# Early picks in one stretch, a plain first slot, K of the third pair over two queues, and one late unit's values in a score buffer

## Chip, cores and metric

The kernel runs on one core of one Trainium2 chip. The metric is the time of one execution on the device in microseconds (us), the median of several runs. Five engines work side by side, each with its own instruction order, and wait for each other through semaphores: PE (TensorE: matmuls into the PSUM accumulators), DVE (VectorE), ACT (ScalarE), POOL (GpSimd) and SP (SyncE, which here only starts transfers). A transfer can be started from the queue of SP, ACT or POOL, and stands there in the same order as that engine's other instructions.

## What is computed

Attention with queries pooled in pairs, and behind it a top-1 mixture of experts. q, k and v are 8 x 8 x 1152 x 64 in float32; there are 8 experts with an inner width of 1024.

```python
q_pool = q.reshape(B, H, S // 2, 2, D).mean(axis=3)          # 576 queries
scores = np.matmul(q_pool, k.transpose(0, 1, 3, 2)) / np.sqrt(D)
attn = np.exp(scores - np.max(scores, axis=-1, keepdims=True))
attn = attn / (np.sum(attn, axis=-1, keepdims=True) + 1e-09)
x = heads_joined(np.matmul(attn, v))                         # 4608 tokens x 512
expert_idx, gate_w = top1(softmax(x @ w_gate))
for e in range(8):
    out[expert_idx == e] = gate_w * (np.maximum(x @ w1[e], 0.0) @ w2[e])
```

## The kernel before

**Attention.** The work is 8 batches x 4 pairs of heads x 2 halves of the queries: 64 units, eight in each batch. For a pair, `load_pair` (L476) loads K (`kp`, four transfers of 144 KB), Q (`qn`) and V (`vn`). Two neighbouring queries are added (`qp`, on POOL at L527 for all pairs but the first), and DVE transposes K and Q in blocks (`kT` L537, `qT` L541). A unit's scores are nine chunks: PE writes one into a score buffer (`st`, L573; there are three such buffers in PSUM), and DVE takes it out with its maximum (L577, a "take"). Behind the ninth chunk come `top` (L598), a small spread on PE (L595) and the `bias` (L601); then ACT makes the exponentials (L605) in five pieces. POOL folds the exponentials for the row sums (L665), PE adds up what is left (L648, L655), and PE multiplies the exponentials by V (`values`, L709) into the one value buffer `pa`. ACT and DVE bring `pa` into `xT` (L715, L717).

**Start.** For the first two pairs (`start`), half of the K and Q transfers go over the queue of ACT (`side`, L488) and half over SP; for all others all go over SP (L487). Every such transfer start waits for one of eight semaphores, which SP and ACT use in turn: a start waits until the transfer that had its semaphore last has landed.

**Routing and slots.** When a batch is done, `routing` (L757) turns its row sums (L725, L732), makes the logits (L787), brings them over on ACT (L808, `sm`), turns them back (L794), weighs them (`lw`, L800) and finds each token's expert. The tokens then go through 16 slots, each for one expert: three early slots, six wide and seven static ones. Behind the next-to-last batch `first_slots` (L911) chooses the three early slots' experts: three picks of twelve small DVE instructions each (L931 to L942). Each pick has a score buffer of its own for its scratch row (`pe`), and in the plan the picks stand some time apart (`K_NEXT * i`).

**A slot.** `turn_tokens` (L1176) weighs gathered tokens (`xt`, L1196), crosses them on PE into `px` (L1204), and splits them into a rounded part `xh` (ACT, L1211) and a rest `xl` (DVE, L1152). `split_weights` (L1230) does so with the weights (`w1h`, `w1l`, `w2h`, `w2l`; casts on ACT at L1243, rests on DVE at L1152). `first_products` (L1261) makes eight blocks of twelve matmuls (L1305) in two buffers `ph`, each emptied into `hh` (ACT, L1313) and `hl` (DVE, L1315), and `second_products` (L1321) multiplies these by `w2` into `py` (L1335).

The first slot is special. The first of its eight blocks is made in three parts (`by_part`, L1291): four matmuls that need only `xh` and `w1h`, four that need also `xl`, and four that need `w1l`. A filler (L1281) keeps PE busy ahead of them. The third cross goes into `py`, so that it doesn't wait for a `px`. Casts of the weights behind the first wait for the `xh`, rests for the `xl`; the logits of the last batch wait for the parts.

**Order.** All of this is laid out by a planner (`Flow`, L95) ahead of time: steps have a key, an estimated duration, steps that must come before them and buffers that they hold, and the planner writes out one fixed order for each engine. A change of a key or a buffer thus changes the order of other work too.

Of the kernel before, what the change touches and what calls it, by code (L numbers as in the profile page):

```python
# [9 lines left out]
F32 = mybir.dt.float32  # L10
# [60 lines left out]
FILLERS = 1  # L71
# [198 lines left out]
def kernel(  # L270
# [151 lines left out]
    def open_attention(exact, base, pairs, units):  # L422
# [10 lines left out]
        o.turned, o.asked, o.gate, o.ended = [], None, None, []  # L433
# [42 lines left out]
    def load_pair(o, f, key, b, hp):  # L476
# [13 lines left out]
        start = not o.exact and b == 0 and hp < 2  # L490

        def quarters(t, src, n0=0, n1=rows, load=load):

            for h in range(2):
                for i in range(D // BL):
                    g = (h * D // BL + i) * BL
                    (side if start and h else load)(t[g:g + BL, n0:n1], src[h][:, i * BL:(i + 1) * BL].rearrange("(p n) d -> p n d", p=BL)[:, n0:n1])

        def k_part(n0, n1, ns, move, after=()):
            return f.carry("SP", ns, lambda: quarters(kp.t, heads(k, b, hp), n0, n1), key + K_LOAD, after, [kp], move)  # L500

        def q_part(n0, n1, ns, move):
            return f.carry("SP", ns, lambda: quarters(
                qn.t.rearrange("p j b t d -> p (j b t) d"), heads(q, b, hp), n0, n1),
# [191 lines left out]
    def values(o, f, key, x, s, ready, hp, half, xT):  # L696
        pa = value_banks(o)
# [18 lines left out]
        o.ended += done(a)  # L716
# [27 lines left out]
    def attend(o, f, key, b, hp, xT, sm, summed):  # L744
# [3 lines left out]
        for half in range(2):  # L748
# [3 lines left out]
            outs.append(values(o, f, at + 10 - (40 if end and half else 0), x, s, r, hp, half, xT))  # L752
# [4 lines left out]
    def routing(o, f, key, b, xT, rec, ready, hold=()):  # L757
# [49 lines left out]
        o.logits = p = f.add("PE", 1050, logits, at, done(o.gate, *ready), [pl, xT], COLS)  # L807
        p = f.add("ACT", act(HQ) - 44, lambda: nc.scalar.copy(lg.t, pl.t[:, 0, :HQ]), at, done(p), [pl, lg])  # L808
# [58 lines left out]
        def put(g):  # L867
# [18 lines left out]
            p = [f.add("ACT", 115, lambda d=d: spread(d), at + K_SPREAD, ready, [rec, row]) for d in range(NQD)]  # L886
            p += [f.add("DVE", dve(NR * P), lambda j=j: turn(j), at + K_PUT * j / NJ / NB, ready, [row, xT]) for j in range(0, NJ, NR)]
# [23 lines left out]
    def first_slots(o, m, f, key, ready):  # L911
# [7 lines left out]
        n, pl8 = small("fn"), small("fpl8")  # L919
        p = f.add("PE", 60, lambda: nc.tensor.matmul(pc.t[0:1, 0, :NE], ones_bf[:, 0:1], cnt, start=True, stop=True),  # L920
# [5 lines left out]
        def pick(i, p):  # L926

            pe = score_banks(o)
            eq = lambda: pe.t[0:1, 1, :NE]
# [577 lines left out]
```

## Time and profile before

| | |
|---|---|
| median of 3 runs | 1147.12 us (1146.98 to 1150.65) |
| the profiled execution | 1160.67 us, of which the span is 1159.0 us |
| PE busy | 1121.1 us, 97% of the span |
| DVE, POOL, ACT busy | 882.6, 846.7 and 619.8 us |
| attention of the 64 units | from the start to about 683 us |
| slots | from about 684 us to the end |

The profiled execution is 13.55 us longer than the median. Times in it are read from its own start; sums of them are set against its own time.

### The profile page before, as it was taken

How to read it: one execution, taken by the hardware profiler on the slowest of the kernel's cores; microseconds unless marked ns; L12 is line 12 of the kernel's file. 1: busy time of each engine (PE TensorE's matmuls, PEld its weight loads, DVE VectorE, ACT ScalarE, POOL GpSimd, SP SyncE). 2: the span in 40 equal slices, each digit the busy share in tenths (PEclk: the TensorE clock that was granted, in tenths of full speed). 3: DMA queues.
4: the chain of work that ended last, by engine and by line, in shares of the span. 5: the costliest groups of instructions: out<-in, count | busy, mean ns of one | idle time of the engine just before them, and what ended most of it. 6: DMA issues, size and time to landing. Idle time of an engine off the chain costs nothing.

```text
span 1159.0 us, 32925 instructions
## 1 busy us (share of the span) xinstructions
PE 1121.1 (97%) x13237; PEld 797.0 (69%) x13237; DVE 882.6 (76%) x2245; ACT 619.8 (53%) x831; POOL 846.7 (73%) x484
## 2 busy tenths in 40 slices
PE   7999999999999999999999989999999999999994
PEld 3555555555555655555555568899999999899894
DVE  7988988989989889898889849755665556677760
ACT  2755656556557456555555555444444444555550
POOL 2999999999999999999999832766655654455510
PEclk9999999999999999999999999999999999999998
DMA  9876757566566566558453347856555555677630
GB/s 139 144 145 122 128 79 129 86 103 115 85 105 122 72 109 126 88 84 139 77 94 82 93 116 183 246 156 196 179 175 157 170 172 184 202 253 240 220 124 14
DMA packets 397977, 158.07 MB, mean 136 GB/s; under 512 B 314310, under 2 KB 368482, under 8 KB 397816
## 3 DMA queue, kind: packets, MB, share of 16 engines
q1 hardware_dynamic: 376696, 133.63, 52.9%
q0 software_dynamic: 10464, 20.78, 5.8%
q10 hardware_dynamic: 10656, 1.48, 1.1%
q8 instruction: 106, 1.74, 0.7%
q14 instruction: 55, 0.45, 0.1%
HBM read 135.02 MB, written 22.07 MB: 136 GB/s over the span
## 4 chain that ended last, share of the span: by engine, by line
PE 69%; DVE 16%; issue 6%; DMA 4%; POOL 2%; ACT 1%; SPq 1%; another core or an unknown queue 0%; POOLq 0%; DVEq 0%; ACTq 0%
PE st L573 18%; PE pa L709 17%; PE ph L1305 15%; PE py L1335 15%; DVE s L577 8%; PE st L655 2%; DMA vn<-in_v_dram 2%; DVE kT L537 2%; PE st L648 1%; DVE row L877 1%; POOL fold L665 1%; DMA qn<-in_q_dram 1%; PE st L595 1%; SPq L487 1%; POOL out_dram L1344 1%
## 5 line engine op out<-in xcount | busy, mean ns | idle before, releaser
L605 ACT ACTIVATE s<-s,bias 128x1152 f32<-128x1152 f32 (+1 forms) x320 | 352.0, 1152 | 242.2 <-DVE bias L601 218.3
L577 DVE TENSOR_SCALAR_CACHE_REDUCE s<-st 128x576 f32<-128x576 f32 x576 | 417.2, 748 | 48.4 <-PE st L573 33.1
L573 PE MATMUL st<-qT,kT 64*64 64x288 f32 x4608 | 366.3, 409 | 12.4 <-DVE s L577 7.8
L709 PE MATMUL pa<-s,vn 64*64 64x288 f32 x4608 | 350.1, 404 | 1.6 <-DVE xT L717 1.1
L573 PEld LDWEIGHTS st<-qT,kT 64*64 64x64 f32 x4608 | 165.1, 133 | 138.0 <-DVE s L577 57.0
L709 PEld LDWEIGHTS pa<-s,vn 64*64 64x64 f32 x4608 | 175.5, 133 | 105.9 <-issue 8.7
L665 POOL TENSOR_TENSOR fold<-s 128x1728 f32<-128x1728 f32 x55 | 213.0, 3874 | 17.4 <-ACT s L605 15.5
L665 POOL TENSOR_TENSOR fold<-fold,s 128x1728 f32<-128x1728 f32 x55 | 213.1, 3876 | 1.5
L1305 PE MATMUL ph<-xh,w1h 128*128 128x372 f32 (+1 forms) x508 | 155.7, 306 | 0.5 <-DVE hl L1315 0.5
L1305 PE MATMUL ph<-xl,w1h 128*128 128x372 f32 (+1 forms) x508 | 155.4, 306 | 0.0
L1305 PE MATMUL ph<-xh,w1l 128*128 128x372 f32 (+1 forms) x508 | 154.6, 304 | 0.0
L1152 DVE TENSOR_TENSOR w2l<-raw,w2h 128x1024 fp32r<-128x1024 f32 x64 | 78.1, 1224 | 84.9 <-ACT w2h L1243 76.1
L1021 POOL DMA_INDIRECT xr<-x_runs,ix x76 | 89.4, 1177 | 54.4 <-issue 24.8
L1335 PE MATMUL py<-w2h,hh 128*128 128x512 f32 x328 | 128.1, 391 | 0.0
L1335 PE MATMUL py<-w2h,hl 128*128 128x512 f32 x328 | 127.8, 390 | 0.0
L1335 PE MATMUL py<-w2l,hh 128*128 128x512 f32 x328 | 127.8, 390 | 0.0
L1313 ACT ACTIVATE hh<-ph 128x372 fp32r<-128x372 f32 (+1 forms) x100 | 51.1, 511 | 107.3 <-PE ph L1305 94.3
L1344 POOL DMA_INDIRECT out_dram<-y,rec x41 | 43.4, 1058 | 84.8 <-ACT y L1352 64.4
L1021 POOL DMA_INDIRECT xq<-x_runs,ix x52 | 63.4, 1219 | 49.0 <-PE py L1335 26.5
L1305 PEld LDWEIGHTS ph<-xh,w1h 128*128 128x128 f32 x508 | 95.4, 188 | 2.0 <-DVE hl L1315 0.8
L1305 PEld LDWEIGHTS ph<-xl,w1h 128*128 128x128 f32 x508 | 95.4, 188 | 0.6
L1305 PEld LDWEIGHTS ph<-xh,w1l 128*128 128x128 f32 x508 | 95.2, 187 | 0.0
(225 smaller groups left out, 1331.8 us busy)
## 6 DMA issues: line engine op xcount, KB each, us to landing
raw<-in_moe_w_dram SPq DMA_DIRECT2D x128, 512.0 KB
vn<-in_v_dram SPq DMA_DIRECT2D x124, 144.0 KB
kp<-in_k_dram SPq DMA_DIRECT2D x122, 144.0 KB
qn<-in_q_dram SPq DMA_DIRECT2D x120, 144.0 KB
x_runs<-row SPq DMA_DIRECT2D x96, 99.0 KB
xr<-x_runs,ix POOLq DMA_INDIRECT x76
x_runs<-empty SPq DMA_DIRECT2D x4, 297.0 KB
xq<-x_runs,ix POOLq DMA_INDIRECT x52
```

What stands on the lines that cost most here:

```text
L537: nc.vector.transpose(view(kT.t.rearrange(f"p (c b i) -> p {order} i", b=NQD, i=BL)), view(kp.t.rearrange(f"p ({order}) d -> p {order} d", ...
L573: nc.tensor.matmul(pt.t[to, h, :HQ], x.kT.t[up, c * P + i * D:c * P + (i + 1) * D], x.qT.t[up, cols], start=True, stop=True, tile_position ...
L577: nc.vector.tensor_scalar(s.t[:, c], pt.t[:, :, :HQ], -SCALE, None, op0=ALU.mult, op1=ALU.min, accum_out=mx.t[:, c:c + 1],)
L605: nc.scalar.activation(s.t[:, c0:c0 + n], s.t[:, c0:c0 + n], AF.Exp, bias=bias.t, scale=-1.0)
L665: add = lambda to, a, b: nc.gpsimd.tensor_tensor(to, a, b, ALU.add)
L709: mark.made = nc.tensor.matmul(pa.t[cs, i, :HQ], x.vn.t[up, h, c, :], s.t[up, c, h], start=c == 0, stop=c == NC - 1, tile_position=(up.sta ...
L1021: ins = nc.gpsimd.indirect_dma_start(out=x.xr[i // NQD].t[:, i % NQD, :], out_offset=None, in_=xg, in_offset=bass.IndirectOffsetOnAxis(ap= ...
L1152: (nc.gpsimd if eng == "POOL" else nc.vector).tensor_tensor(lo, raw, hi.bitcast(F32), ALU.subtract)
L1305: mark.made = nc.tensor.matmul(view()[:, i, :], a[:, c, fp], b[:, c, :n], start=c == 0 and k == 0, stop=c == NDC - 1 and k == 2)
L1313: a = f.add("ACT", act(nb * n) - 44, lambda home=home, apart=apart: nc.scalar.activation(home(0), apart(), AF.Relu), at - 20, done(p), [ph ...
L1335: mark.made = nc.tensor.matmul(py.t, blocks(a)[:, c * x.nr + r], b[:, c % 2, :], start=c == 0 and k == 0, stop=c == NFC - 1 and k == 2)
L1344: ins = nc.gpsimd.indirect_dma_start(out=out, out_offset=bass.IndirectOffsetOnAxis(ap=x.re.t.bitcast(I32)[:, r, 0:1], axis=0), in_=y.t, in ...
```

## The change

- **Picks.** The three picks write their scratch row into the buffer `pc` that holds the count they start from, and have one key.
- **First slot.** The parts, the filler, the third cross in `py` and the special waits are gone; all eight blocks are ordinary ones.
- **Third pair.** The transfers of K for the third pair (`third`: batch 0, pair 2) go half over ACT, half over SP. Its Q stays on SP.
- **Late values.** The values of the last unit go into a score buffer instead of `pa`.
- **Small things.** Two copies that pad `hh` and `hl` go from DVE to POOL, and the copies of the last batch's `rec` (L872) stand behind the copy of its logits (`copied`).

```diff
@@ load_pair
         start = not o.exact and b == 0 and hp < 2
+        third = not o.exact and b == 0 and hp == 2
...
-                    (side if start and h else load)(t[g:g + BL, n0:n1], src[h][:, i * BL:(i + 1) * BL].rearrange("(p n) d -> p n d", p=BL)[:, n0:n1])
+                    (side if both and h else load)(t[g:g + BL, n0:n1], src[h][:, i * BL:(i + 1) * BL].rearrange("(p n) d -> p n d", p=BL)[:, n0:n1])
 
         def k_part(n0, n1, ns, move, after=()):
-            return f.carry("SP", ns, lambda: quarters(kp.t, heads(k, b, hp), n0, n1), key + K_LOAD, after, [kp], move)
+            return f.carry("SP", ns, lambda: quarters(kp.t, heads(k, b, hp), n0, n1, start or third), key + K_LOAD, after, [kp], move)
...
-            move = 3800 if start else 4600 if not o.exact and b == 0 and hp == 2 else 2600
-            k0 = [k_part(0, rows, 620 if start else 1900, move, done(o.asked))] * 2
+            move = 3800 if start else 4600 if third else 2600
+            k0 = [k_part(0, rows, 620 if start else 950 if third else 1900, 3800 if third else move, done(o.asked))] * 2
@@ values, attend
-    def values(o, f, key, x, s, ready, hp, half, xT):
-        pa = value_banks(o)
+    def values(o, f, key, x, s, ready, hp, half, xT, banks):
+        pa = banks(o)
...
-            outs.append(values(o, f, at + 10 - (40 if end and half else 0), x, s, r, hp, half, xT))
+            outs.append(values(o, f, at + 10 - (40 if end and half else 0), x, s, r, hp, half, xT,
+                               score_banks if end and half else value_banks))
@@ routing
+            if b == B - 1:
+                f.order([copied], p)
@@ first_slots
+        eq = lambda: pc.t[0:1, 1, :NE]
...
-            pe = score_banks(o)
-            eq = lambda: pe.t[0:1, 1, :NE]
...
-            return f.add("DVE", 2300, lambda: [fn() for fn in fns], key + K_NEXT * i, done(p), [pe])
+            return f.add("DVE", 2300, lambda: [fn() for fn in fns], key, done(p), [pc])
@@ turn_tokens, split_weights, hidden
-                bank = "py" if x.begins and r == 2 else "px"
-                px = hold_of(bank, lambda h, bank=bank: m.ps.tile([P, DM], F32, **h.own(bank)))
+                px = hold_of("px", lambda h: m.ps.tile([P, DM], F32, **h.own("px")))
...
-            rows = x.casts if x.begins and (j or not one) else ()
-            lows = x.lows[:None if j or not one else 2] if x.begins else ()
...
-                nc.vector.tensor_copy(blocks(t)[:, :, RT:], ones4[:, 0, 0, 4:4 + P - RT].unsqueeze(1)
+                nc.gpsimd.tensor_copy(blocks(t)[:, :, RT:], ones4[:, 0, 0, 4:4 + P - RT].unsqueeze(1)
@@ first_products
-            if x.begins and f0 == 0:
...
-                p = f.add("PE", 430 * FILLERS, fill, at - 45, x.crossed, [filled])
...
-                    needs = ((*x.w1_ready[0][:1], *x.casts), x.lows, x.w1_ready[0])[k]
...
-            for i in range(0 if x.begins and f0 == 0 else nb):
+            for i in range(nb):
@@ the slots
-            if i == 0:
-                f.order(x.casts[-1:], [max(o.ended)])
-                f.order(done(x.parts), done(o.logits))
-            if i == 1:
-                f.order(slots[0].lows, x.put)
```

What it does to the order, at three places. First ACT at the start of the program, from the last transfers of the second pair (`qn`) to the second unit's exponentials (L605, `s`). Before:

```order
L488 DMA kp_233<-in_k_dram 32x36x32 x2
L488 DMA qn_295<-in_q_dram 32x18x32 x4
L605 ACTIVATE s_254<-s_254,bias 128x1152 x4
L605 ACTIVATE s_254<-s_254,bias 128x576
L605 ACTIVATE s_328<-s_328,bias 128x1152 x4
L605 ACTIVATE s_328<-s_328,bias 128x576
```

After:

```order
L487 DMA kp_233<-in_k_dram 32x36x32 x2
L487 DMA qn_295<-in_q_dram 32x18x32 x4
L487 DMA kp_336<-in_k_dram 32x36x32 x2
L605 ACTIVATE s_254<-s_254,bias 128x1152 x4
L605 ACTIVATE s_254<-s_254,bias 128x576
L605 ACTIVATE s_328<-s_328,bias 128x1152 x4
L605 ACTIVATE s_328<-s_328,bias 128x576
```

The two transfers of the third pair's K (`kp_336`) stand on ACT ahead of the program's first exponentials; on SP two are left.

Second DVE at the picks, late in the attention: from the end of the first pick (`head`) to the start of the second (`ffm`). Before:

```order
L942 TENSOR_TENSOR head<-head,st_8895 1x8
L577 TENSOR_SCALAR s_8790,mx<-st_8875 128x576
L577 TENSOR_SCALAR s_8790,mx<-st_8913 128x576
L577 TENSOR_SCALAR s_8954,mx<-st_8936 128x576
L598 TENSOR_REDUCE top<-mx 128x1
L931 TENSOR_REDUCE ffm<-fn 1x1
L932 TENSOR_SCALAR st_8971<-fn,ffm 1x8
```

After:

```order
L943 TENSOR_TENSOR head<-head,st_8872 1x8
L577 TENSOR_SCALAR s_8790,mx<-st_8875 128x576
L932 TENSOR_REDUCE ffm<-fn 1x1
L933 TENSOR_SCALAR st_8872<-fn,ffm 1x8
L934 TENSOR_TENSOR st_8872<-st_8872,rev 1x8
```

One take stands between the picks where three takes and `top` stood; the third pick follows in the same way, and `top` stands behind it.

Third PE from the last values of the attention to the first slot (`ph`). Before:

```order
L648 MATMUL st_9459<-s_9218,ones_73 32x288 x18
L709 MATMUL pa_9480<-s_9108,vn_8817 64x288 x20
L725 MATMUL st_9510<-ones 128x128 x3
L732 MATMUL st_9510<-sums_of,sm_8774 96x16 x3
L709 MATMUL pa_9480<-s_9108,vn_8817 64x288 x16
L1204 MATMUL px_9583<-ident,xt_9579 128x128 x4
L1204 MATMUL px_9588<-ident,xt_9581 128x128 x4
L1204 MATMUL py_9604<-ident,xt_9597 128x128 x4
L1281 MATMUL ph_9609<-ones_73,ones 128x512
L1291 MATMUL ph_9618<-xh,w1h_9576 128x372 x4
L1291 MATMUL ph_9618<-xl,w1h_9576 128x372 x4
L1291 MATMUL ph_9618<-xh,w1l_9577 128x372 x4
```

After:

```order
L709 MATMUL st_9381<-s_9221,vn_8817 64x288 x24
L709 MATMUL pa_9424<-s_9099,vn_8817 64x288 x4
L709 MATMUL st_9381<-s_9221,vn_8817 64x288 x12
L709 MATMUL pa_9424<-s_9099,vn_8817 64x288 x32
L648 MATMUL st_9487<-s_9099,ones_73 32x288 x18
L648 MATMUL st_9508<-s_9221,ones_73 32x288 x18
L724 MATMUL st_9529<-ones 128x128 x3
L731 MATMUL st_9529<-sums_of,sm_8774 96x16 x3
L787 MATMUL pa_9540<-xT_8669,wg 32x288 x8
L1203 MATMUL px_9602<-ident,xt_9591 128x128 x4
L1203 MATMUL px_9611<-ident,xt_9596 128x128 x4
L1203 MATMUL px_9631<-ident,xt_9623 128x128 x4
```

All values now stand ahead of the sums' turn (L731); the logits (L787), which stood among the products, stand ahead of the crosses; behind the crosses follow L794 and the first block of products, without filler and parts.

## Rows read from the trace of the kernel before

**Rows 1.** The page: busy time of each engine, with share of the span and instructions.

```profile
PE 1121.1 (97%) x13237; PEld 797.0 (69%) x13237; DVE 882.6 (76%) x2245; ACT 619.8 (53%) x831; POOL 846.7 (73%) x484
```

**Rows 2.** Busy time by stretch; columns: window, length, busy (instructions), PEclk, DMA, GB/s.

```profile
30.00:60.00 30.00, 27.81 (x448) 15.41 (x444) 27.56 (x81) 21.37 (x23) 30.00 (x12) 1.00 0.86 151
60.00:620.00 560.00, 554.14 (x8990) 323.79 (x8986) 497.38 (x1478) 331.21 (x441) 532.84 (x215) 1.00 0.62 105
```

**Rows 3.** Timeline of ACT's queue and of SP's at the start; columns: start, duration.

```profile
15.35 5.49 ACTq L488 DMA_DIRECT2D qn<-in_q_dram  x4
20.52 0.32 ACTq L488 DMA_DIRECT2D qn<-in_q_dram  x1
20.89 5.36 ACT L605 ACTIVATE s<-s,bias 128x1152 f32<-128x1152 f32 x5 [18.43 <-DMA qn<-in_q_dram]
...
21.76 0.31 SPq L487 DMA_DIRECT2D vn<-in_v_dram  x1
23.69 0.57 SPq L487 DMA_DIRECT2D kp<-in_k_dram  x1
```

**Rows 4.** Timeline of POOL, the same stage.

```profile
24.52 3.87 POOL L665 TENSOR_TENSOR fold<-s 128x1728 f32<-128x1728 f32 x1 [0.30 <-ACT s L605]
28.36 0.79 POOL L527 TENSOR_TENSOR qp<-qn 128x288 f32<-128x288 f32 x1
...
52.35 1.42 POOL L527 TENSOR_TENSOR qp<-qn 128x576 f32<-128x576 f32 x1
```

**Rows 5.** Timeline of DVE and PE, the same stage.

```profile
29.94 0.47 DVE L541 STREAM_TRANSPOSE qT<-qp 128x288 f32<-128x288 f32 x1
33.70 0.58 DVE L537 STREAM_TRANSPOSE kT<-kp 128x384 f32<-128x384 f32 x1
53.80 0.84 DVE L541 STREAM_TRANSPOSE qT<-qp 128x288 f32<-128x288 f32 x2 [0.39 <-POOL qp L527]
35.98 0.34 PE L595 MATMUL st<-ident,top 64*64 64x64 f32 x8 [1.42 <-DVE s L577]
```

**Rows 6.** Timeline at the picks, PE and DVE.

```profile
639.06 0.34 PE L595 MATMUL st<-ident,top 64*64 64x64 f32 x8 [0.49 <-DVE head L942]
637.06 0.14 DVE L931 TENSOR_REDUCE ffm<-fn 1x1 f32<-1x8 f32 x1
638.77 0.14 DVE L942 TENSOR_TENSOR head<-head,st 1x8 f32<-1x8 f32 x1
```

**Rows 7.** Busy time (columns as in rows 2) from the last score to the first slot's end.

```profile
663.30:728.40 65.10, 61.19 (x546) 47.57 (x547) 45.03 (x114) 32.28 (x54) 21.99 (x21) 1.00 0.57 152
```

**Rows 8.** Timeline of PE from the last values into the first slot.

```profile
672.64 4.69 PE L709 MATMUL pa<-s,vn 64*64 64x288 f32 x72 [1.07 <-DVE xT L717]
683.17 0.60 PE L732 MATMUL st<-sums_of,sm 128*96 128x16 f32 x6
685.81 1.09 PE L1204 MATMUL px<-ident,xt 128*128 128x128 f32 x8
687.74 1.02 PE L1281 MATMUL ph<-ones,ones 128*128 128x512 f32 x2
688.57 0.94 PE L1291 MATMUL ph<-xh,w1h 128*128 128x372 f32 x4
690.52 0.95 PE L1291 MATMUL ph<-xl,w1h 128*128 128x372 f32 x4 [1.01 <-DVE xl L1152]
695.83 1.18 PE L787 MATMUL pa<-xT,wg 128*32 128x288 f32 x16
699.92 0.53 PE L794 MATMUL pa<-ident,sm 128*96 128x128 f32 x3 [0.71 <-ACT sm L808]
```

**Rows 9.** Timeline of DVE at the first slot.

```profile
684.42 1.22 DVE L1196 TENSOR_TENSOR xt<-xr 128x512 f32<-128x512 f32 x2
690.38 3.48 DVE L1152 TENSOR_TENSOR w1l<-raw,w1h 128x1024 fp32r<-128x1024 f32 x3
```

**Rows 10.** Busy time (columns as in rows 2) right after the program's start.

```profile
8.00:10.00 2.00, 2.00 (x20) 1.07 (x16) 0.85 (x3) 0.00 (x0) 0.00 (x0) 0.50 1.54 150
```

More of the change, by code (lines that the diff above doesn't have):

```diff
@@ L432, in open_attention @@
         o.exact, o.marks = exact, []
-        o.turned, o.asked, o.gate, o.ended = [], None, None, []
+        o.turned, o.asked, o.gate = [], None, None
         return o
@@ L490, in load_pair, with quarters @@
         start = not o.exact and b == 0 and hp < 2
-        def quarters(t, src, n0=0, n1=rows, load=load):
+        third = not o.exact and b == 0 and hp == 2
+        def quarters(t, src, n0, n1, both):
             for h in range(2):
@@ L715, in values @@
         a = f.add("ACT", act(HQ) - 44, lambda: nc.scalar.copy(xT.t[:, hp, to], pa.t[:, 0, :HQ]), key + 20, done(p), [pa, xT])
-        o.ended += done(a)
         return f.add("DVE", 100 + dve(HQ), lambda: nc.vector.tensor_tensor(
@@ L805, in weigh @@
                 )
-        o.logits = p = f.add("PE", 1050, logits, at, done(o.gate, *ready), [pl, xT], COLS)
-        p = f.add("ACT", act(HQ) - 44, lambda: nc.scalar.copy(lg.t, pl.t[:, 0, :HQ]), at, done(p), [pl, lg])
+        p = f.add("PE", 1050, logits, at, done(o.gate, *ready), [pl, xT], COLS)
+        p = copied = f.add("ACT", act(HQ) - 44, lambda: nc.scalar.copy(lg.t, pl.t[:, 0, :HQ]), at, done(p), [pl, lg])
         p = f.add("PE", 330, turn, at, done(p), [pt, lg])
@@ L1176, in turn_tokens @@
     def turn_tokens(o, m, f, x, key):
-        x.casts, x.lows, x.put, x.crossed = [], [], [], []
         n, nb = x.n, x.nb
@@ L1207, in turn_tokens @@
                 p = f.add("DVE", dve(DM), across, key + r, x.rows[r:r + 1], [xt, x.xr[r]])
-                x.put += done(p)
                 p = f.add("PE", 450, cross, key + r, done(p), [x.x, px, xt])
-                x.crossed += done(p)
                 a = f.add("ACT", act(DM) - 44, lambda rs=rs, made=made: nc.scalar.copy(x.x.t[0][:, :, rs], made()),
@@ L1215, in turn_tokens @@
                 x.turned += done(a, d)
-                x.casts += done(a)
-                x.lows += done(d)
                 continue
@@ L1240, in split_weights @@
             e = "POOL" if pool_bits >> j & 1 else "DVE"
-            rows = x.casts if x.begins and (j or not one) else ()
-            lows = x.lows[:None if j or not one else 2] if x.begins else ()
             a = f.add("ACT", act(1024), lambda j=j, src=src: nc.scalar.copy(w[j].t[0], src()),
-                      key + step * j, done(got[j], *rows), [raw[j], w[j]])
+                      key + step * j, done(got[j]), [raw[j], w[j]])
             d = f.add(e, (pool if e == "POOL" else dve)(1024), lambda j=j, e=e, src=src: low(e, w[j].t[1], src(), w[j].t[0]),
-                      key + step * j, done(a, *lows), [raw[j], w[j]])
+                      key + step * j, done(a), [raw[j], w[j]])
             ready.append(done(a, d))
@@ L1276, in first_products @@
             p = None
-            if x.begins and f0 == 0:
-                def fill():
-                    for _ in range(FILLERS):
-                        nc.tensor.matmul(filled.t, ones, ones4.rearrange("p a b c -> p (a b c)").unsqueeze(1).broadcast_to([P, 2, 256]), start=True, stop=True)
-                filled = hold_of("ph", lambda h: m.ps.tile([P, 512], F32, **h.own("ph")))
-                p = f.add("PE", 430 * FILLERS, fill, at - 45, x.crossed, [filled])
-                for k in range(3):
-                    def by_part(k=k, view=view):
-                        (wh, wl), (xh, xl) = x.w1[0].t, x.x.t
-                        a, b = ((wh, xh), (wh, xl), (wl, xh))[k]
-                        for c in range(NDC):
-                            nc.tensor.matmul(view()[:, 0, :], a[:, c, :P], b[:, c, :n],
-                                             start=c == 0 and k == 0, stop=c == NDC - 1 and k == 2)
-                    needs = ((*x.w1_ready[0][:1], *x.casts), x.lows, x.w1_ready[0])[k]
-                    x.parts = p = f.add("PE", NDC * (0.436 * n + 6), by_part, at, done(p, *needs), [ph, x.x, x.w1[0]])
-            for i in range(0 if x.begins and f0 == 0 else nb):
+            for i in range(nb):
                 for c0 in range(0, NDC, 2):
@@ L1408 @@
         order += [((etab, rtab), i, T) for i in range(STATIC_SLOTS)]
-        base, marks, slots = key + K_SLOT, [], []
+        base, marks = key + K_SLOT, []
         for i, (tab, s, n) in enumerate(order):
```

6 lines of the change are left out of this document (1 added, 5 removed).

## Prediction

> **What bounds the kernel now.** I read the page first, then the busy times by stretch, then the timelines of the places that the change touches. PE is busy 1121.1 us of a span of 1159.0 [rows 1]; from 60 to 620 us it is 554.14 of 560, POOL 532.84 of 560 [rows 2]. So nearly all of the span is a queue of matmuls, and a change moves the end only by pauses of PE that it makes or takes away. Such pauses are at three places: in the first 60 us, at the picks, and between the attention and the slots. Whatever is lost ahead of 60 us stays lost, since there is hardly any pause behind it that could give it back. In the first 60 us it isn't PE that leads: from 30 to 60 us POOL is busy 30.00 of 30 us, DVE 27.56 and PE 27.81 [rows 2], so there is no slack on POOL at all.
>
> **The third pair's K.** What it can gain: SP starts the four transfers from 23.69 us on, and DVE first reads that K at 33.70 with no wait named in its row [rows 3, 5]. K has thus 10 us, and landing sooner is worth nothing.
>
> What it costs stands on ACT. The two starts come ahead of the first exponentials, which began at 20.89, straight behind ACT's last start at 20.52 (0.32 us) [rows 3]. A start waits until the transfer before it on its semaphore has landed. By the order of the semaphores, the first of the new starts waits for the same transfer as SP's start of V at 21.76 did, the second for the same as SP's first start of this K at 23.69 [rows 3]. The first is therefore free by 21.76 at the latest; the second at some time up to 23.69, when it was started at once. With 0.31 to 0.57 us for a start [rows 3], the exponentials begin between about 22.4 (both free when ACT comes to them) and 24.3. That is 1.5 to 3.4 us late. I take 2.8, near the upper end, because the transfers ahead land one behind the other at this time.
>
> Who waits for that: POOL's first fold started 0.30 us behind the exponentials that it adds, at 24.52, and behind it on POOL stands `qp` at 28.36 (0.79 us), so it ended at 29.15 [rows 4]. It now ends at 29.15 + 2.8 = 31.95. DVE transposes it at 29.94 [rows 5]: DVE waits 31.95 - 29.94 = 2.0 us. PE's products with the late exponentials stand among scores, so PE is held too, but that falls in the same time. POOL, full, stays 2.8 late. Its `qp` at 52.35 (1.42 us) ended at 53.77, and DVE waited for it already, 0.39 us up to 53.80 [rows 4, 5]; DVE, 2.0 late, waits another 2.8 - 2.0 = 0.8. There DVE has some slack (497.38 busy of the 560 us from 60 on [rows 2]), and I count half of it. Sum: 2.0 + 0.4 = **+2.4 us**. Bounds: 0, if both starts are free at once and the 1.5 us is lost in the three score buffers; 3.4, if all of the delay reaches PE.
>
> The Trainium skill speaks to this in "DMA: Bandwidth & Descriptors", section "Issuing engines are not separate DMA queues": transfers started from several engines interleave on the same 16 DMA engines, and a second engine saves only the time to start them, "usually small relative to the DMA itself". That the transfer gains nothing agrees with the row. But by that rule the price on ACT would be two short starts, an estimate of 2 x 0.32 = 0.64 us and a sum that is 1.8 us lower, where the row shows that four starts took ACT 5.49 us [rows 3]. I go by the row.
>
> **Picks.** A pick takes from 637.06 to 638.77 + 0.14 = 638.91, some 1.8 us [rows 6]. The twelve instructions remain; two of three scratch buffers are saved, and PE's spread at 639.06 waited 0.49 us for a pick [rows 6]. Now the third pick too stands ahead of `top`, so this unit's bias comes about 1.1 us later (1.8 less a take of 0.7 that stood ahead of it), and the next unit's about 2.9 sooner. Stepping the takes and scores to the last score, I get **-0.5 us**; bounds -1.1 (both pauses that lie here gone) and +1.1 (the later bias holds PE).
>
> **Last values.** `pa` is one buffer: PE waited 1.07 us for DVE to empty it [rows 8]. With the last unit's values in a score buffer that wait goes: -1.07. The 16 values matmuls behind the sums' turn only move ahead of it.
>
> **First slot.** From the last score at 663.3 to the first slot's end at 728.4 PE wasn't busy for 65.10 - 61.19 = 3.91 us [rows 7]; without the 1.07 of `pa` that is 2.84, in pauses of which the largest are 1.01 for `xl` and 0.71 for the logits' copy [rows 8]. All of these go, since the steps are laid out anew: -2.84. The filler, from 687.74 to 688.57 [rows 8], goes as well: -0.83. What comes instead I step from the time T at which the sums' turn (L731) ends. DVE: the reciprocals to T+0.65 (from 683.17 + 0.60 to 684.42 before [rows 8, 9]), two `xt` of 0.61 each to T+1.9 [rows 9], then `w1l` of the first weights, 3.48 / 3 = 1.16 [rows 9], to T+3.05, and only then the third `xt`, to T+3.7. PE: logits to T+1.1, two crosses (1.09 for both) at T+1.3 and T+1.9 [rows 8]; the third waits for its `xt` and for the `px` that the first `xl` frees, T+4.3. The last `xl`, behind another `w1l`, is there at T+6.7. The first block needs it from its second matmul on, where before four matmuls that need no `xl` stood ahead. So work of 3.0 us (logits 1.1, crosses 1.6, L794 0.3 [rows 8]) takes 6.7: a pause of +3.7. The third block then waits for `hl`, which stands on DVE behind two more `w1l`: +0.75. The fourth waits for an `hh` that stands on ACT behind a cast whose raw weights must land first: +1.15. A last wait is +0.1. Sum: -2.84 - 0.83 + 3.7 + 0.75 + 1.15 + 0.1 = +2.0, and with the last values -1.07 + 2.0 = **+1.0 us**. Bounds: -2.5, if the two late waits (1.9) don't come and the long pause is 1.6 shorter because the third cross finds a free `px`; +3.0, if each of the two late waits is 1 us longer.
>
> The two padding copies (0.2 us each of DVE) go to POOL, which has room there; nothing else is late for it. The copies of `rec` are moved on ACT behind the logits copy, into time in which ACT waits for casts; 0 either way, and 1 us if the third `hh` stands behind them, which is in the bound above.
>
> **Sum.** 2.4 - 0.5 + 1.0 = +2.9 us on the profiled execution: 1160.67 + 2.9 = 1163.6. The profiled execution lies 13.55 us over the median; the places named here lie in the stretch that both have in common, and I put the same difference on the median: 1147.12 + 2.9 = **1150.0**. Taking the bounds that can fall together, 0 - 1.1 - 1.5 = -2.6 and 3.4 + 0 + 2.5 = +5.9: 1144.5 to 1153.0.
>
> **Rivals.**
>
> *Faster: the early delay doesn't happen, and a pause goes.* At 35.98 PE waited 1.42 us for a buffer that DVE had to take [rows 5], because `top` and K's transposes stood between takes. The new order puts K's transposes ahead of the last takes and the spread one product later. If the starts on ACT are free when ACT comes to them, the early term is -1.4 instead of +2.4, and with the slot at its better end (-1.5) the sum is -1.4 - 0.5 - 1.5 = -3.4: 1143.7. For it: K is there in time. Against it: DVE, busy 27.56 of 30 us there [rows 2], has no room for its order to gain PE much, and the rows of SP say that the semaphores were not free.
>
> *Slower: PE's clock falls in the first slot's pauses.* Early in the program, where PE waits for its first transfers, PE's granted clock was 0.50 from 8 to 10 us, that is the 1.2 GHz level [rows 10]. At the change between attention and slots the longest pause before is 1.07 us [rows 8] and the clock stays at 1.00 [rows 7]; now there are pauses of 1.9 us (third cross) and 1.5 us (`xl`) close together. At that level a matmul takes twice as long; if it lasts for the third cross and most of the first block, 2.0 us of matmuls take 4.0: +2.0, in all +4.9: 1152.0. It decides if the two pauses together are enough for the clock to fall. "TensorE: Matmul & The Clock Gate", section "HAM oscillation", in the Trainium skill says that a kernel whose matmul bursts are parted by waits falls back to the low clock burst by burst; that speaks against taking the filler out, and by it this rival would be the rule.
>
> *It doesn't do what it says.* ACT's new starts are not held, POOL's fold is on time, and the slot's pauses cancel: -0.5 to 0, 1146.9.
>
> **How the numbers follow.** A measurement of this kernel tells 0.3%, 3.4 us, from no change: faster is below 1143.7, slower above 1150.6. Forecast 0.45, of which 0.27 lie within and 0.18 slower (its middle is just below the bound, and the bounds reach as far up as down); faster rival 0.17, of which 0.09 faster and 0.08 within; slower rival 0.18, all slower but 0.03; nothing done 0.20, within but for 0.02 faster. Together: faster 0.11, within 0.56, slower 0.33. The range leaves out one in ten at either side: 1144.0 to 1153.0.
>
> **What would show it.** In the profile after: ACT's first exponentials at 22.4 to 24.3 instead of 20.89, POOL's first fold at 26 to 28, a wait of DVE's `qT` for `qp` of some 2 us near 30; at 53 to 58 a longer wait for `qp`. At the picks no wait of PE's spread for `head`. At the end of the attention no wait of L709 for `xT`, and from the sums' turn to the second matmul of the first block some 6.7 us, with clock 1.00. It is wrong if the exponentials start on time, if the first block starts within 4 us of the sums' turn, or if a place outside these three moves by more than 1 us.

## The result

The changed kernel takes 1157.93 us (median of 8 runs, 1153.99 to 1159.3), the kernel before, on the same chip, 1149.93 (8 runs, 1146.98 to 1150.99). The ratio is 1.0069, with a 95% interval of 1.0059 to 1.0079: slower by some 8.0 us. The prediction was +2.9 us, with bounds up to +5.9. The sign was right; the size and the range were not.

The profiled execution of before is longer than its usual run, and its trace shows where: from the end of one batch to the end of the next it took 81.7 to 84.1 us (the last one aside), where the changed kernel took an even 81.5. So the two spans are not compared below, only places. First the page of the changed kernel, busy time of each engine; it answers to [rows 1].

```profile
PE 1123.6 (97%) x13235; PEld 805.4 (70%) x13235; DVE 883.0 (76%) x2243; ACT 619.2 (54%) x831; POOL 852.0 (74%) x486
```

PE works 2.5 us longer on two instructions fewer. This is no more than a hint that matmuls have become slower somewhere, since the two executions differ in the middle. The timelines show where.

**The start.** ACT's queue in the changed kernel, a timeline (start, duration), against [rows 3]:

```profile
20.67 3.10 ACTq L487 DMA_DIRECT2D kp<-in_k_dram  x2
23.82 5.36 ACT L605 ACTIVATE s<-s,bias 128x1152 f32<-128x1152 f32 x5 [21.37 <-DMA qn<-in_q_dram]
```

PE at the same time:

```profile
19.64 1.78 PE L573 MATMUL st<-qT,kT 64*64 64x288 f32 x24
25.12 1.64 PE L709 MATMUL pa<-s,vn 64*64 64x288 f32 x8 [3.70 <-ACT s L605]
26.14 1.58 PE L573 MATMUL st<-qT,kT 64*64 64x288 f32 x8
27.10 1.58 PE L709 MATMUL pa<-s,vn 64*64 64x288 f32 x8
```

The two starts held ACT for 3.10 us and the exponentials began 2.93 us late. PE, whose next matmul is the first product with V, stood still for 3.70 us. Groups of eight matmuls then start some 1.0 us apart, where before they did 0.5 apart:

```profile
26.89 0.67 PE L709 MATMUL pa<-s,vn 64*64 64x288 f32 x8
27.38 0.67 PE L573 MATMUL st<-qT,kT 64*64 64x288 f32 x8
```

The table of the changed kernel by stretches says why (length, busy time of PE, PEld, DVE, ACT, POOL with instructions, granted clock of PE, DMA share and GB/s):

```profile
22.00:24.00 2.00, 0.00 (x0) 0.00 (x0) 0.86 (x3) 0.18 (x1) 0.78 (x1) 1.00 1.17 175
24.00:26.00 2.00, 0.88 (x7) 0.88 (x11) 1.68 (x5) 2.00 (x2) 0.00 (x0) 0.53 1.01 199
26.00:28.00 2.00, 2.00 (x22) 2.00 (x18) 0.24 (x1) 2.00 (x3) 0.56 (x1) 0.50 0.88 110
28.00:30.00 2.00, 2.00 (x23) 2.00 (x19) 0.53 (x2) 1.18 (x2) 2.00 (x1) 0.50 0.50 76
```

Behind the pause PE's granted clock is 0.50, the 1.2 GHz level, until past 30 us. DVE, which had been nearly full there, is busy 0.24 of 2 us: it now waits for scores. The sums' turn that ends batch 0 starts 5.1 us later, first before, then changed:

```profile
109.65 0.68 PE L732 MATMUL st<-sums_of,sm 128*96 128x16 f32 x6
114.79 0.68 PE L731 MATMUL st<-sums_of,sm 128*96 128x16 f32 x6
```

How much of that reaches the end, these two traces can't say; the runs below do.

**The products of the slots.** In the chain of work that ended last, one slot's 96 first products are one piece (start, duration). Before:

```profile
797.19 16.01 PE ph L1305 x96
829.57 16.01 PE ph L1305 x96
```

The changed kernel:

```profile
791.01 16.32 PE ph L1279 x96
823.70 16.32 PE ph L1279 x96
```

The same products, back to back at full clock, take 166.8 ns each before and 170.0 after. The 248-column slots go from 10.89 to 11.20 us a slot in the same way. Sixteen slots at 0.31 us are 5.0 us, at a place that the change doesn't name at all.

The reason is not in the order of instructions but in the place of a tile. The tiles of the slots get their place in SBUF when the code first asks for them. In the planner's new order two tiles of gathered tokens (`xq_1`, `xq_2`) are asked for ahead of `xh`, so that by the allocation of the built kernel `xh` lies at byte 214944 of its partition instead of 210720, and `xl` behind it. The weights `w1h0` stay at 196320. (That the place is the cause is shown only by the experiments.)

**The end of the attention and the first slot.** PE in the changed kernel, against [rows 8]:

```profile
679.88 0.60 PE L731 MATMUL st<-sums_of,sm 128*96 128x16 f32 x6
680.41 1.18 PE L787 MATMUL pa<-xT,wg 128*32 128x288 f32 x16
681.90 1.16 PE L1203 MATMUL px<-ident,xt 128*128 128x128 f32 x8 [0.31 <-DVE xt L1196]
684.81 0.63 PE L1203 MATMUL px<-ident,xt 128*128 128x128 f32 x4 [1.75 <-DVE xl L1153]
685.27 0.49 PE L794 MATMUL pa<-ident,sm 128*96 128x128 f32 x3
686.10 0.52 PE L1279 MATMUL ph<-xh,w1h 128*128 128x372 f32 x1 [0.33 <-ACT xh L1208]
687.01 0.68 PE L1279 MATMUL ph<-xl,w1h 128*128 128x372 f32 x1 [0.39 <-DVE xl L1153]
687.49 0.51 PE L1279 MATMUL ph<-xh,w1l 128*128 128x372 f32 x1
687.80 0.51 PE L1279 MATMUL ph<-xh,w1h 128*128 128x372 f32 x1
...
694.74 0.44 PE L1279 MATMUL ph<-xh,w1h 128*128 128x372 f32 x1 [0.30 <-DVE hl L1289]
```

This is nearly the step that was worked out: from the sums' turn's end (680.41) to the second product 6.6 us, predicted 6.7. The late waits (0.75 and 1.15 predicted) shrank to one of 0.30. In their place the clock fell: products start 0.31 us apart from 687.5 to 689.7 us, then 0.17.

### The profile page after: what moved, and what is told of

It reads as the page before. It is cut to its first block, busy times and chain, and to the rows that moved or that the text cites. A ratio compares the mean times of both kernels' runs of the same rounds, so it can differ in the third digit from the quotient of the medians.

```text
span 1156.2 us, 32927 instructions
## 1 busy us (share of the span) xinstructions
PE 1123.6 (97%) x13235; PEld 805.4 (70%) x13235; DVE 883.0 (76%) x2243; ACT 619.2 (54%) x831; POOL 852.0 (74%) x486
## 5 line engine op out<-in xcount | busy, mean ns | idle before, releaser
L605 ACT ACTIVATE s<-s,bias 128x1152 f32<-128x1152 f32 (+1 forms) x320 | 352.1, 1152 | 245.0 <-DVE bias L601 212.0
L709 PE MATMUL pa<-s,vn 64*64 64x288 f32 x4536 | 346.2, 406 | 3.7 <-ACT s L605 3.7
L709 PEld LDWEIGHTS pa<-s,vn 64*64 64x64 f32 x4536 | 173.2, 134 | 107.2 <-DVE xT L716 7.4
L1279 PE MATMUL ph<-xh,w1h 128*128 128x372 f32 (+1 forms) x512 | 159.2, 311 | 0.6 <-ACT xh L1208 0.3
L1279 PE MATMUL ph<-xl,w1h 128*128 128x372 f32 (+1 forms) x512 | 159.1, 311 | 0.4 <-DVE xl L1153 0.4
L1279 PE MATMUL ph<-xh,w1l 128*128 128x372 f32 (+1 forms) x512 | 159.0, 310 | 0.0
L1022 POOL DMA_INDIRECT xr<-x_runs,ix x76 | 95.8, 1260 | 49.9 <-issue 25.9
```

The lines of the kernel that those rows point to most:

```text
L605: nc.scalar.activation(s.t[:, c0:c0 + n], s.t[:, c0:c0 + n], AF.Exp, bias=bias.t, scale=-1.0)
L709: mark.made = nc.tensor.matmul(pa.t[cs, i, :HQ], x.vn.t[up, h, c, :], s.t[up, c, h], start=c == 0, stop=c == NC - 1, tile_position=(up.sta ...
L1022: ins = nc.gpsimd.indirect_dma_start(out=x.xr[i // NQD].t[:, i % NQD, :], out_offset=None, in_=xg, in_offset=bass.IndirectOffsetOnAxis(ap= ...
L1279: mark.made = nc.tensor.matmul(view()[:, i, :], a[:, c, fp], b[:, c, :n], start=c == 0 and k == 0, stop=c == NDC - 1 and k == 2)
```

## Experiments

Ratios are to the kernel before in the same comparison, and losses in us are worked out from them. The medians alone would give up to 1.7 us less or more (the kernel before took 1149.63 us beside the first four kernels), so that is how far a single loss can be trusted.

Theory at this point: +8 us is about half the transfers on ACT (the late start and the clock behind it), half the place of `xh` and `xl`, and the rest of the change is worth next to nothing. The rivals: the late start alone is the whole cost of the transfers; the products' rate depends on the PSUM banks, which also changed, or on the order of instructions; the first slot costs what the transfers don't.

**The third pair's K on SP alone, all else changed.**

```diff
-        third = not o.exact and b == 0 and hp == 2
+        third = False
...
```

> The changed kernel with one part undone: the third pair's K goes over SP alone again; everything else of the change stays, and the order differs from the changed kernel's only in some ten rows of the first 60 us. Theory A (the K starts on ACT cost the early time): the first exponentials begin near 20.9 us again instead of 23.82, the second unit's near 28.6 instead of 33.74, the clock stays at 1.00 from 15 to 30 us, and the time falls by 5.1 us against the changed kernel, that is about +2.9 us (1.0025) against the kernel before. Theory B (the early delay is absorbed later, by pauses or waits between 60 and 620 us): the exponentials come early as well, but the time stays within 1.5 us of the changed kernel's, +6.5 to +9.5 us against the kernel before. My blind sum had this part at 2.4 us.

1153.12 us, ratio 1.0038 (1.0025 to 1.0050). The exponentials begin on time, and the clock is 1.00 in all of the first 30 us:

```profile
20.32 5.37 ACT L605 ACTIVATE s<-s,bias 128x1152 f32<-128x1152 f32 x5 [17.86 <-DMA qn<-in_q_dram]
```

Of the 8.0 us 3.6 are gone: theory A, though less than the 5.1 that it expected. What is left are products of 170.0 ns.

**K over both queues alone, in the kernel before.** The edits of `load_pair` from the diff, and nothing else.

> The kernel before with one part of the change alone: two of the four transfers of the third pair's K start from ACT's queue. Theory A: +5.1 us against the kernel before (1.0044), first exponentials at 23.8, the clock at 1.2 GHz for some 6 us behind the pause. Theory B: 0 to +1.5 us. My blind sum: +2.4.

1153.38 us, 1.0045 (1.0026 to 1.0064): +5.2 us (by the medians +3.8). PE's row, and the stretches behind it:

```profile
25.63 1.39 PE L710 MATMUL pa<-s,vn 64*64 64x288 f32 x7 [4.30 <-ACT s L606]
```

```profile
26.00:28.00 2.00, 2.00 (x21) 1.93 (x20) 0.00 (x0) 2.00 (x3) 0.06 (x1) 0.50 1.22 168
28.00:30.00 2.00, 2.00 (x28) 1.95 (x25) 0.77 (x2) 1.67 (x2) 2.00 (x1) 0.67 0.79 81
```

**The changed kernel with the tiles at the places of before.** The tiles are asked for in the old order right where the pools are opened; the order of instructions on each engine and the PSUM banks are those of the changed kernel.

```diff
             add_moe(m, units, "tile", side="right")
+            m.x.tile([P, NDC, P], F32, name="xt_0", bufs=1)
+            m.x.tile([P, NDC, P], F32, name="xt_1", bufs=1)
+            m.x.tile([P, NQD, RUN], F32, name="xq_0", bufs=1)
+            m.x.tile([P, NDC, TW], F32R, name="xh", bufs=1)
+            m.x.tile([P, NDC, TW], F32R, name="xl", bufs=1)
...
```

> The changed kernel with not one instruction moved: the tiles of the slots' tokens are laid out in SBUF in the order of the kernel before (xh at 210720 instead of 214944 bytes, xl at 216864 instead of 221088, the buffers xt and xq around them), nothing else. In the changed kernel a product of the slots (128x372) follows the next every 0.1700 us, in the kernel before every 0.1667 us. Theory C (where xh and xl lie sets the products' rate): 0.1667 again, and with some 1536 products of either width 1536 x 3.4 ns = 5.2 us less than the changed kernel, so about +2.8 us against the kernel before. Theory D (the PSUM banks of the products, which also moved, from 5 and 6 to 4 and 5, or a slower rate of this run's chip): 0.1700 stays, time like the changed kernel's, +8.

1153.96 us, 1.0034 (1.0020 to 1.0048). A slot's products in the chain:

```profile
822.84 16.01 PE ph L1279 x96
```

**The kernel before with the tiles at the new places.** The same in the other direction; order and banks of before.

> The kernel before, not one instruction moved, with the tiles of the slots' tokens laid out in SBUF as in the changed kernel (xh at 214944, xl at 221088 bytes); the PSUM banks stay 5 and 6. Theory C (place in SBUF): products every 0.1700 us and +5.2 us against the kernel before (1.0045). Theory D (banks, or the chip): products every 0.1667 us, no change.

1153.63 us, 1.0041 (1.0028 to 1.0055): +4.7 us by where two tiles lie.

```profile
818.50 16.32 PE ph L1305 x96
851.18 16.32 PE ph L1305 x96
```

Two orders and two sets of banks, and in all four kernels the rate follows the place. That settles the second half.

**Which place?** Two kernels, each executed once, so that only their rates are read. A pad of 128 unused bytes moves both tiles and the weights in the one, and the weights alone in the other.

> The kernel before with 128 unused bytes behind the token tiles: xh, xl and the weights w1 all lie 128 bytes lower (xh at 210592, w1h0 at 196192), their distance is unchanged. If the distance of tokens and weights sets the products' rate: steps of 160 and 170 ns as before (mean 166.7). If the absolute place does (xh 32 bytes behind a multiple of 256 before, now 160, as in the changed kernel): 170 ns for all three kinds of step.

> The kernel before with 128 unused bytes ahead of xh: xh and xl stay where they were, the weights w1 lie 128 bytes lower. If the absolute place of xh and xl sets the rate: 160 and 170 ns as before (mean 166.7). If the distance between tokens and weights does: another pattern.

Moved together, the slot's products take as long as before; with the weights alone moved, as long as in the changed kernel. First the one, then the other:

```profile
799.89 16.01 PE ph L1305 x96
```

```profile
792.99 16.32 PE ph L1305 x96
```

So it is how the moving tile lies to the weights, not where either lies. A kernel of products alone measures that directly: blocks of 24 matmuls with the moving tile set off in steps of 32 bytes, at four places of the weights. It computes nothing of the attention or the experts.

> A kernel of products alone: nothing of the attention and the experts is computed. It runs the twelve matmuls of a block of first products (order, strides and float32r as in the kernels) 24 at a time without a wait, with the moving tile (xh, xl) set off from the weights' tile by 0 to 480 bytes in steps of 32, at four places of the weights (0, 64, 128, 192 bytes), for 372 columns, and at one place of the weights for 368, 248 and 512 columns. Theory P (the distance of the two tiles): in the four placements run so far the step was 166.7 ns where xh lies 64 bytes behind a multiple of 256 from w1h0 (14400 bytes, twice), and 170.0 ns where it lies 192 behind (14528 and 18624 bytes). P expects the step to depend on that distance modulo 256 alone: at 64 and 320 bytes of distance 166.7, at 192 and 448 170.0, the same at all four places of the weights. Theory A (the place of each tile on its own, for instance by where the moving rows begin): the pattern over the moving tile's offset is the same at all four places of the weights and doesn't shift with them. Theory N (not the place, but what else reads and writes SBUF beside PE): all steps of 372 columns alike, since nothing else runs here. A distance with less than 166.7 would be a better place than that of before.

Two pieces of its timeline (start, duration of 24; the step is the distance of the starts over 24). The weights are set off by 128 bytes in the first four rows, up to 217.70:

```profile
177.04 4.16 PE L41 MATMUL pb<-x,w 128*128 128x372 f32 x24
181.04 4.24 PE L41 MATMUL pa<-x,w 128*128 128x372 f32 x24
...
209.62 4.16 PE L41 MATMUL pb<-x,w 128*128 128x372 f32 x24
213.62 4.24 PE L41 MATMUL pa<-x,w 128*128 128x372 f32 x24
217.70 4.16 PE L41 MATMUL pb<-x,w 128*128 128x372 f32 x24
221.70 4.24 PE L41 MATMUL pa<-x,w 128*128 128x372 f32 x24
```

The block at 177.04 (moving tile at 192, weights at 128: distance 64) has a step of 4.00 / 24 = 166.7 ns, the next one (distance 96) 4.08 / 24 = 170.0. The fast ones come back at 209.62 (distance 320) and, with the weights at 192, at 217.70 (distance -192, that is 64 modulo 256). At the distances of 64 modulo 256 all eight blocks have 166.7 to 167.5 ns; of the other 56, two (distance 32) have 167.1 and 54 have 169.2 to 171.3. Theory P holds for the two distances that the kernels have (64 and 192 modulo 256), A and N fall. But the distance isn't all of it: at 32 the two blocks of 167.1 have the weights at 0 and 64, and with the weights at 128 and 192 the same distance has 170.8. No block is under 166.7: the kernel before already had the better place, so there is no gain to fetch here. For 512 columns 227.9 to 229.2 ns stand at distances of 0 and 64 modulo 256, 232.9 to 234.2 elsewhere. For 368 columns the pattern is another: 165.8 ns at 128 and 172.9 at 384, which are the same modulo 256. So the rule is one for 372 columns, and each other width has to be measured.

**What of the transfers' cost is the clock?** The kernel with K over both queues alone, with fillers on PE in the pause ahead of the first product with V, five and then three.

```diff
-            def product(c=c, mark=mark):
...
+            def product(c=c, mark=mark, lead=not o.exact and not o.marks):
...
+                if lead:
+                    for _ in range(5):
+                        nc.tensor.matmul(pa.t[:, 1], ones, ones.unsqueeze(1).broadcast_to([P, 4, P]), start=True, stop=True)
```

> The kernel before with K on ACT alone (as in the run e2_k_alone, +5.2 us), and with five filler matmuls of 128x512 on PE ahead of the first unit's first product with V, where PE stands idle for 3.7 us waiting for the late exponentials. The fillers leave the exponentials as late as they are (23.8 us). Theory E (half of the early loss is the clock, which falls to 1.2 GHz in that pause): the clock stays at 1.00 from 15 to 30 us, the second unit's exponentials begin near 31.4 instead of 33.7, and the time comes out at +2.4 to +3.0 us against the kernel before, near my blind sum. Theory F (the delay passes through POOL and ACT whatever the clock is): the time stays at +4.5 to +5.5.

> Before, with K of the third pair over both queues alone, and three fillers (128x512, 0.91 us each by the run with five) in PE's pause ahead of the first product with V. With five, PE's clock stayed at 1.00, but the fillers ended at 26.04 us, some 2.3 us behind the time (22.42 + 1.30 us) at which the first exponentials allowed the product, and the time was 1.0048 of before. Theory E (the pause matters by the fall of PE's clock behind it): with fillers to about 24.2 us the clock stays at 1.00 or nearly so, no or little time is overrun, and the loss is 2 to 3 us, ratio 1.002 to 1.003; the third unit's exponentials come 16.0 to 16.8 us behind the first ones. Theory F (the late exponentials alone cost it, through POOL's folds and DVE's order, the clock hardly): ratio 1.004 to 1.005 as with no and with five fillers, and the third unit's exponentials 17.7 to 18.0 us behind the first ones, where before they are 15.5 to 16.0.

Five: 1.0048 (1.0029 to 1.0067), no gain, as theory F expected. Its timeline shows another cause:

```profile
21.48 4.56 PE L709 MATMUL pa<-ones 128*128 128x512 f32 x10
25.97 0.72 PE L713 MATMUL pa<-s,vn 64*64 64x288 f32 x8
```

The clock stayed at 1.00, but a filler took 0.91 us, and five ended some 2.3 us after the exponentials allowed the product (begun at 22.42, plus 1.30). So they can have cost what they saved. Three:

```profile
21.40 2.84 PE L709 MATMUL pa<-ones 128*128 128x512 f32 x6
24.17 0.72 PE L713 MATMUL pa<-s,vn 64*64 64x288 f32 x8
24.70 0.67 PE L574 MATMUL st<-qT,kT 64*64 64x288 f32 x8
```

1150.99 us beside 1148.71 of before, 1.0020 (1.0011 to 1.0029). The third unit's exponentials come 16.1 us behind the first (22.55 to 38.66), as before (20.89 to 36.84: 16.0), not 17.7 (24.32 to 42.03) as without fillers. Theory E. From the first exponentials to the sums' turn of batch 0 it is 88.3 us with three fillers and 88.3 to 88.8 in seven executions where K stays on SP, but 89.9 and 90.0 in two without fillers (K over both queues alone; the changed kernel with the old places), and 91.0 in the changed kernel. (Three more with K on SP, from comparisons in which the batches were long, have 89.4 to 90.5, so this is no sharp measure.) So the late start of ACT goes through in full, and pause and low clock add 1.1 to 2.7 us to it. (By the times the fillers give back 2.9 us, but the two kernels ran in different comparisons, and ACT's first exponentials began at 22.55 in the one and at 24.32 in the other, so part of that is the execution.)

**Both undone: what the rest is worth.** The changed kernel with K on SP and the tiles at their old places, in three comparisons; and twice with two fillers (128x448) in PE's pause ahead of the first slot's third cross.

> The changed kernel with the third pair's K on SP alone and the slots' token tiles at the places of the kernel before: what is left of the change are the picks, the plain first slot, the last unit's values and the small things. If the two causes found so far (K on ACT +0.45%, places +0.41%) add up, what is left is 0.69 - 0.45 - 0.41 = -0.17%, that is -2.0 us against the kernel before, though my blind sum for it was -0.5 + 1.0 = +0.5. If they don't add up (a shared cause), it stays at +0.2 to +0.4%.

> The changed kernel with the third pair's K on SP alone and the tiles at the places of before, as run once already (ratio 1.0012, 0.9993 to 1.0032), again beside the kernel before and the filled one. The rest of the change (picks, plain first slot, last values in a score buffer) should be within 0.2% of before: the sum that was forecast for it was -0.5 + 1.0 = +0.5 us (1.0004); if the parts measured alone add up (3.5 us for the transfers, 4.0 for the places, 8.0 for the whole), it is +0.5 us too. Above 1.002 there would be a third cost that isn't named yet; below 0.999 the rest would gain.

> The same kernel without the fillers, for the third time (1.0012 and 0.9980 so far, each with an interval of 0.4%). Forecast of the rest of the change: +0.5 us, ratio 1.0004. The difference to the filled kernel should be 0 to 1.3 us: 1.3 in executions in which PE's clock falls in the first slot (three of five profiled so far), 0 in the others.

> The changed kernel with the third pair's K on SP alone and the tiles at the places of before, and two fillers (128x448, an estimate of 0.80 us each from 0.91 us for 128x512) in PE's pause of 1.75 us ahead of the third cross of the first slot. Without them PE's clock fell there: the first products took 0.31 us each from 690.11 to 692.28 us instead of 0.17, some 1.3 us in all. Theory H (the pauses made the clock fall, and that is what the plain first slot costs): the clock stays at 1.00 from 684 to 694 us, the first block's steps are 0.17 us, and the time is 1.0 to 1.5 us under that of the same kernel without the fillers: ratio to before 0.999 to 1.0005. Theory G (the clock falls by itself at this place, for instance by the wait for xl and xh of 0.3 to 0.5 us behind, or the fillers only push the third cross back): steps of 0.31 us remain, or PE reaches the first block later by as much as is saved; ratio as without the fillers.

> The same kernel as the filled one before (both parts undone, two fillers in the first slot's pause). On a chip where the kernel before takes about 1149 us the spread is a third of that of the last comparison. If picks, plain first slot and last values are worth what the last comparison said (0.9971, 0.9950 to 0.9991), the ratio is again below 0.999; if they cost the forecast +0.5 us less at most 1.3 us for the clock, it is 0.999 to 1.0005.

| | both undone | and filled |
|---|---|---|
| first (before 1159.20 us) | 1.0012 (0.9993 to 1.0032) | |
| second (before 1163.31) | 0.9980 (0.9960 to 1.0000) | 0.9971 (0.9950 to 0.9991) |
| third (before 1148.57) | 0.9997 (0.9988 to 1.0006) | 0.9994 (0.9985 to 1.0003) |

The third, with the smallest spread, says -0.3 us (-1.4 to +0.7) for picks, plain first slot and last values together. No third cost shows. The fillers can't be told from no effect: 0.9971 was not found again. Nor did the clock fall each time. Behind the same pauses (0.31, 1.75, 0.33, 0.2 to 0.5 us) it fell in the executions profiled of the changed kernel, of the one with old places, and of the first and third here; it did not in the one with K on SP, nor in the second here. With fillers it stayed at 1.00 in both executions, which is too few to show that they hold it. In the third the products started 0.31 us apart from 682.2 to 687.4 us:

```profile
682.48 0.51 PE L1279 MATMUL ph<-xh,w1h 128*128 128x372 f32 x1
682.80 0.51 PE L1279 MATMUL ph<-xl,w1h 128*128 128x372 f32 x1
```

There the third slot's products began 78.9 us behind the sums' turn, against 77.7 with fillers. In two other pairs, one execution with the fall and one without, the difference is 0.5 us each (changed kernel and K on SP, 78.5 and 78.0; first and second here, 80.5 and 80.0). So the fall cost 0.5 to 1.2 us where it came, and whether it came differed from execution to execution.

## Where the prediction was right and where it failed

**The third pair's K: right in its first steps, wrong in the one that sets the cost.** The exponentials came 2.93 us late (2.8 predicted), POOL's first fold at 27.44 (26 to 28). The closeness is in part luck: where K stays on SP they began anywhere from 19.57 to 20.90 us, and the trace of before, at 20.89, was one of the latest. But the term stood at +2.4, and runs give 3.6 (taken out of the changed kernel), 5.2 (put alone into the kernel before) and 4.2 (old places, 1.0034, less both undone, 0.9997). The step that failed is the sentence that PE is held too, "but that falls in the same time". PE's next instruction in its queue was the product with V itself. It stood for 3.70 us, and then the clock was at 1.2 GHz for 6 us. The predicted wait of DVE's `qT` for `qp` did not come, nor did the longer one in the fifties (that `qT`, at 53.80 before, is at 58.46 and names no wait):

```profile
31.25 0.79 POOL L527 TENSOR_TENSOR qp<-qn 128x288 f32<-128x288 f32 x1
35.07 0.47 DVE L541 STREAM_TRANSPOSE qT<-qp 128x288 f32<-128x288 f32 x1
```

DVE waited for PE instead:

```profile
27.76 0.76 DVE L577 TENSOR_SCALAR_CACHE_REDUCE s<-st 128x576 f32<-128x576 f32 x1 [2.08 <-PE st L573]
30.64 0.76 DVE L577 TENSOR_SCALAR_CACHE_REDUCE s<-st 128x576 f32<-128x576 f32 x1 [2.11 <-PE st L573]
```

POOL, which the prediction took as full, ran out of work as well, 1.50 us ahead of the second unit's folds, since those exponentials came 5.1 us late.

The clock's fall was a rival, but only for the first slot. [rows 10] had shown the low level behind a wait of PE at the program's start (2.06 us, by the timeline of before, up to 7.77); the same question should have been asked of the 2.8 us that the sum itself had just put between PE and its next product. One reading was also loose: with both starts free when ACT came to them, the rows give 20.84 + 2 x 0.32 = 21.5 us for the exponentials, not 22.4, which is the time with the first start held to 21.76.

By the Trainium skill, "DMA: Bandwidth & Descriptors", section "Issuing engines are not separate DMA queues", a second issuing engine saves only the usually small time to start a transfer; at the 0.32 us of a row of before, two starts would have cost ACT an estimated 0.64 us, where the row shows 3.10 us, so going by the row was right. The Trainium skill, "TensorE: Matmul & The Clock Gate", section "HAM oscillation", says that a kernel whose bursts of matmuls are shorter than the waits between them falls back to the low clock at every burst. The pause of 3.70 us with the clock of 0.50 behind it agrees. For the short pauses of the first slot, where the prediction called it the rule, the trace doesn't bear it out as one: four executions of six.

**The products' rate: a step that is missing.** +4.0 to +4.7 us (changed kernel with and without old places; kernel before with new places), 5.0 by the chain. The prediction compared the order of instructions, the banks and the waits, not the places of tiles. It had named the sign that would prove it wrong, a place outside the three that moves by more than 1 us, and this was it. A list of the two programs' allocations would have shown that `xh` moved, but nothing in the trace of before tells that this has a price.

**Picks, last values, first slot: the sum right within what can be measured, in part by luck.** Forecast -0.5 + 1.0 = +0.5 us, measured -0.3 (-1.4 to +0.7). The spread doesn't wait for a pick (636.11), though one score does, 1.07 us; L709 doesn't wait for `xT`; the pause is 6.6 us long. Inside the slot's term two errors work against each other: the late waits were 0.3 instead of 1.9 us, and the clock, the rival, took 0.5 to 1.2 where it fell.

**The sum.** 4.2 (transfers) + 4.5 (places) - 0.3 (rest) = 8.4 us, measured 8.0. The parts come from different comparisons, each good to a us or two, so the agreement says that no large part is missing, and no more. The range ended at 1153.0 because its bounds came from queues and waits; it had nothing in it for a low clock at the start or for a slower rate of the slots' products.

## What to carry to other kernels

- When a step comes later, ask which instruction stands next in each waiting engine's queue; for PE, price the pause and what its clock does behind it. A few dummy matmuls in such a pause can take back about half of the loss, as long as they don't run far past the data: here three gave back some 2 us, five nothing.
- A transfer's start is not free on an engine that computes: if it must wait for a semaphore, everything behind it in that queue waits too.
- Where tiles get their place when first asked for, a new order of steps moves tiles. Fix the places by hand before comparing two orders, or the comparison measures the places.

## What the runs showed of the hardware that was not expected

- The step of back-to-back float32r matmuls (128x372) at full clock depends on the distance of the moving tile from the weights in the partition: 166.7 to 167.5 ns at 64 bytes modulo 256, 169.2 to 171.3 at nearly all others that were tried; 113.4 against 116.7 ns for 248 columns in the kernels, 228 to 229 against 233 to 234 for 512 in the sweep, at other distances for 368. The two sets of PSUM banks made no difference (166.8 and 170.0 ns with either). Why, no run here shows.
- PE's clock fell to 1.2 GHz behind one pause of 3.54, 3.70 or 4.30 us, in each of the three executions profiled that have one. Behind a row of pauses of which the longest was 1.76 us it fell in four executions of six.
